# All differences of the experts' weights on DVE, and the token order spread over earlier steps

## The chip, the core and the metric

The kernel runs on one core of a Trainium2 chip. A core has a matrix engine (PE), three engines for elementwise work (DVE, ACT and POOL), a queue engine (SP) that issues most transfers, and 16 DMA engines. Each engine takes its instructions in the order in which they were written for it; a semaphore holds an instruction until what it needs is done, and everything behind it on that engine waits with it. The metric is the time of one execution in microseconds, the lower the better: 811.08 us is the median of three runs before the change.

## The reference, cut to what matters

```python
attn = softmax(scale * q @ k.T + alibi, causal, window=128)        # 4 x 8 heads x 576 x 64, fp32
x    = (attn @ v) as 2304 tokens x 512
e    = argmax(x @ w_gate)                                           # one of 8 experts per token
y    = gate * sigmoid(x @ w_output_gate)[e] * (relu(x @ w1[e]) @ w2[e])     # 512 -> 1024 -> 512
out  = (silu(y @ w_gate2) * (y @ w_val2)) @ w_out2                  # 512 -> 1536 -> 512, its weights are float64
```

All is computed to fp32 accuracy. Matmuls use a narrower format (fp32r), so each factor is split into a high part (a rounded copy) and a low part (the value minus its high part), and three products are added: high by high, high by low, low by high.

## The kernel before, in words

There are four stages: attention with the routing (to about 132 us of the span), a short stage of tables that sorts the experts by load, eight experts (145 to 381 us), and the last three matrices, called the wide stage (from 381 us).

The experts are numbered p = 0 to 7 by falling load. They take 384, 384, 352, 336, 304, 272, 256 and 256 tokens (the columns of their matmuls). Experts 0 to 6 run in one loop of 16 steps each: steps m = 0 to 7 make one eighth of the hidden layer each (12 matmuls into `oh`, L1441; ACT writes the high part `hh` with a Relu, L1449; DVE the low part `hl`, L1455), steps kk = 0 to 7 add one eighth of the second layer (12 matmuls into `oy`, L1465). Expert 7 does the same from lines of its own (`oh` L1235, `hl` L1247). In the steps kk = 0 to 5, `turn_step` makes the next expert's input: DVE transposes four blocks of tokens (`t<-xr`, L1090), ACT makes their high parts `xh` (L1097) and DVE their low parts `xl` (L1087); the block k is transposed at kk = k, and its `xl` stands at kk = k + 2, ahead of that step's other work. Expert 0's input is made with PE transposes instead (`emit_xT`; its `xl` is L1068). The first matmuls of an expert read all four blocks of `xh` and then all four of `xl`.

Behind each step, `behind_step` does two further jobs on the same engines:

- **Weights of the next expert and of the wide stage.** A *row* is a 128x512 block of an expert's weights: ACT makes its high part (L461) and the low part is a subtraction (L463), on POOL for every third row and on DVE for the others. 112 rows are done there, 37 of them on POOL. A *wide block* is a 128x256 block of float64, brought to fp32 by two ACT instructions (L405, L406) and two of DVE (L412, L417). From expert 1 on there is one row in each step and one wide block in each even step. Both come through a ring of seven staging tiles (`raw`, `rawd`), and SP issues the next load when one is given back.
- **One portion of the token order, in every second step.** `token_order` is a generator of 40 portions of small DVE instructions. Portions 1 to 29 make the list of where each token's result belongs; portions 15, 21 and 27 are six small PE matmuls each (`oid_ps`, L947), which read what DVE wrote in the portions 11 to 13, 17 to 19 and 23 to 25. Portions 30 to 40 make the tables for tokens over an expert's capacity; the last two issue a transfer from ACT's queue that waits for DVE (L1009, L1014). Portion k stands behind the loop's step 2k, counted from 1 over all experts: portion 40 is behind step 80, the last of expert 4.

The order on each engine is the order in which the program writes it (`manual_schedule`), so a portion or a row that is written earlier runs earlier on its engine.

Of the kernel before, what the change touches and what calls it, by code (L numbers as in the profile page):

```python
# [14 lines left out]
ALU = mybir.AluOpType  # L15
# [131 lines left out]
def attn_moe_glu_kernel(ctx, tc, q, k, v, w_gate, w_ogate, w1, w2, w2_gate, w2_val, w2_out, out, caps=CAPS):  # L147
    nc = tc.nc
# [65 lines left out]
    with ExitStack():  # L214
# [32 lines left out]
        def keep_warm(pool, tag, n):  # L247
# [11 lines left out]
            out=ident, in_=ident, pattern=[[-1, 128]], compare_op=ALU.is_equal, fill=0.0, base=0, channel_multiplier=1  # L259
# [29 lines left out]
        for h in range(H):  # L289
            nc.vector.tensor_scalar(  # L290
                out=bias[:, h, :], in0=dist, scalar1=-(2.0 ** (-8.0 * (h + 1) / H)) / scale, scalar2=None, op0=ALU.mult
# [97 lines left out]
        STEPS = 2 * KF  # L389
# [37 lines left out]

        wide_go = [False]

        loaded, halves, lows, n_rows = [], [], [], [0]  # L430
        sorted_known = [False]

        def w_load(most=LA):
# [23 lines left out]
        def w_item(eng):  # L457
            name, kk, c, t = loaded.pop(0)
            if c is None:
                s = slot_of(name, kk)  # L460
                nc.scalar.activation(out=s[:, 0, :], in_=t, func=AF.Copy)  # L461
                n_rows[0] += 1
                (nc.gpsimd if n_rows[0] % 3 == 0 else nc.vector).tensor_tensor(  # L463
                    out=s[:, 1, :], in0=t, in1=s[:, 0, :], op=ALU.subtract
                )
                wt[name + (kk,)] = s
            else:
                fp = 2 * name[2] + c
                if fp == len(wraw):
                    wraw.append(wB[0].tile([128, 2, 2 * KD, 128], I32, tag="wx", name="wraw", bufs=NX))  # L470
                narrow_merge(*narrow_act(t), wraw[fp][:, :, AT[name[0]][kk], :])
            w_load()
# [369 lines left out]
        def scratch():  # L842
# [5 lines left out]
        TT, TS, STT, RED = (  # L848
            nc.vector.tensor_tensor, nc.vector.tensor_scalar, nc.vector.scalar_tensor_tensor, nc.vector.tensor_reduce)
# [204 lines left out]
        def emit_xT(p, kks=range(KD)):  # L1054
            if p >= E:
                return
            n = caps[p]
            cb = -(-n // 128)
            r = xr[p]
            if p not in xe:  # L1060
                xe[p] = [grid(t, KD, n) for t in pair_tile(xe_p, "x", KD * cap)]
            xh, xl = xe[p]
            for kk in kks:
                t = ps_m.tile([128, CP], F32, tag="m", name="tx")
                for c in range(cb):
                    nc.tensor.transpose(t[:, c * 128:c * 128 + 128], features(r[:, c, 0:DM], kk), ident)
                nc.scalar.activation(out=xh[:, kk, :], in_=t[:, 0:n], func=AF.Copy)
                TT(out=xl[:, kk, :], in0=t[:, 0:n], in1=xh[:, kk, :], op=ALU.subtract)  # L1068
# [45 lines left out]
        step_no = [0]  # L1114
# [7 lines left out]
        def behind_step(i0=0):  # L1122
            for i in range(i0, len(plan[step_no[0]])):
                behind_item(i)
            step_no[0] += 1
            if step_no[0] % 2 == 0:
                next(tokens, None)

        UW = 2 * WU
# [294 lines left out]
        with tc.issue_after(last_cnt[0]):  # L1424
            keep_warm(ps_m, "m", 48)
        with tc.manual_schedule(engines=ALL_ORDERED):
            emit_xT(0)
            load_x(1)
            assert wn[0] == 8 and not loaded
            w_load()  # L1430
            tokens = token_order()
            for p in range(E - 1):
                n = caps[p]
                xh, xl = xe.pop(p)
# [1 line left out]
                for m in range(KF):  # L1436
                    o = ps_m.tile([128, cap], F32, tag="m", name="oh")
                    i = 0
                    for a, b in PASSES:
                        for kk in range(KD):  # L1440
                            nc.tensor.matmul(  # L1441
                                out=o[:, 0:n],
# [19 lines left out]
                for kk in range(KF):  # L1462
                    for d in range(KD):
                        for i, (a, b) in enumerate(PASSES):
                            nc.tensor.matmul(  # L1465
                                out=o[d][:, 0:n],
# [42 lines left out]
        with tc.For_i(0, n_ov, 1) as b:  # L1509
# [10 lines left out]
                out=xs[:, :], out_offset=bass.IndirectOffsetOnAxis(ap=pad[:, 0:1], axis=0), in_=xg[:, :],  # L1520
# [6 lines left out]
                out=w1t, in_=w1[bass.ds(e_r, 1)].rearrange("o (k p) f -> p (o k) f", p=128)  # L1527
# [93 lines left out]
```

## Time and profile before

| | |
|---|---|
| median of 3 runs (lowest, highest) | 811.08 us (810.14, 811.08) |
| the profiled execution, its span | 809.85 us, 808.1 us |
| PE busy | 780.0 us, 97% |
| DVE busy | 669.7 us, 83% |
| ACT busy | 504.9 us, 62% |
| POOL busy | 164.9 us, 20% |
| 16 DMA engines, hardware queue q1 | 45.4% |

The shares are averages over stages with different limits. PE is nearly always busy, so what the time can lose is what PE does not do at its peak: stretches in which it waits, and stretches in which its clock is granted at the lower of its two levels. For each of these one asks which engine ended the wait, and what that engine did in the microseconds ahead of it.

### The profile page before, as it was taken

Reading aid. Unit: us, or ns where it says so; the run is one execution under the profiler, and the core shown is the slowest. Engines: PE = TensorE matmul, PEld = TensorE weight load, DVE = VectorE, ACT = ScalarE, POOL = GpSimd, SP = SyncE. Lnnn points to the kernel's source line nnn. Section 1 sums busy time; section 2 is a strip of 40 time slices with the busy share of each in tenths; the row PEclk is TensorE's granted clock in tenths of the full one; section 3 lists DMA queues with packets and bytes.
Section 4 is the critical chain, followed back from the end, with each engine's and each line's share of the span. In section 5 each row is a group of like instructions: output and inputs, shape, how many; then the busy total and the mean of one; then the engine's idle time right before and its main releaser. Section 6 shows DMA issues by size and latency. Waiting matters only on the chain.

```text
span 808.1 us, 17509 instructions
## 1 busy us (share of the span) xinstructions
PE 780.0 (97%) x6031; PEld 724.3 (90%) x6031; DVE 669.7 (83%) x1771; ACT 504.9 (62%) x1355; POOL 164.9 (20%) x249
## 2 busy tenths in 40 slices
PE   8999998999999999899999999999999999999994
PEld 6888875899999999899899999999999999999993
DVE  7799888498887997889999999999877898777642
ACT  6999972356576657668776766665544665445521
POOL 5467886031121222210000000040000002000003
PEclk9999999999999999899999999999999999999997
DMA  9999943897888878891343321233110113011102
GB/s 183 239 216 301 287 146 119 259 301 247 247 231 265 260 226 251 277 305 45 127 135 105 105 92 52 64 119 131 53 52 27 53 54 131 27 52 53 53 27 81
DMA packets 120815, 121.16 MB, mean 150 GB/s; under 512 B 63634, under 2 KB 79634, under 8 KB 120722
## 3 DMA queue, kind: packets, MB, share of 16 engines
q1 hardware_dynamic: 113184, 106.31, 45.4%
q0 software_dynamic: 2880, 9.48, 3.1%
q10 hardware_dynamic: 4658, 4.20, 1.5%
q8 instruction: 49, 0.80, 0.4%
q14 instruction: 44, 0.36, 0.2%
HBM read 89.23 MB, written 30.73 MB: 148 GB/s over the span
## 4 chain that ended last, share of the span: by engine, by line
PE 50%; issue 33%; DVE 8%; DMA 2%; ACT 2%; POOL 2%; SPq 0%; ACTq 0%; another core or an unknown queue 0%; DVEq 0%; POOLq 0%
PE oh L1441 11%; PE oy L1465 9%; PE pa L1315 7%; PE oo L1338 6%; PE pb L1315 5%; PE o L615 3%; PE s L524 3%; POOL out_dram L1353 2%; PE tp L592 2%; PE tq L498 1%; PE oy L1256 1%; PE oh L1235 1%; DVE p L557 1%; DVE xtok L686 1%; DVE w L463 1%
## 5 line engine op out<-in xcount | busy, mean ns | idle before, releaser
L1338 PE MATMUL oo<-xh,hw 128*128 128x512 f32 x432 | 133.4, 390 | 0.0
L1315 PE MATMUL pa<-w 128*128 128x384 f32 x630 | 127.9, 338 | 0.8 <-ACT wtmp L1176 0.6
L1315 PEld LDWEIGHTS pa<-w 128*128 128x128 f32 x630 | 112.2, 188 | 9.4 <-ACT wtmp L1176 1.3
L1353 POOL DMA_INDIRECT out_dram<-ob,oid x18 | 20.5, 1138 | 419.0 <-ACT ob L1176 293.7
L1465 PE MATMUL oy<-hh,w 128*128 128x384 f32 (+5 forms) x448 | 101.1, 312 | 0.0
L1315 PE MATMUL pb<-w 128*128 128x384 f32 x468 | 94.5, 336 | 0.0
L1338 PEld LDWEIGHTS oo<-xh,hw 128*128 128x128 f32 x432 | 79.6, 188 | 6.4
L1176 ACT ACTIVATE w<-w 128x256 fp32r<-128x256 f32 (+2 forms) x168 | 76.1, 461 | 14.2 <-DVE w L1203 10.5
L463 POOL TENSOR_TENSOR w<-raw,w 128x512 fp32r<-128x512 f32 x37 | 49.9, 1348 | 170.2 <-ACT w L461 117.5
L1338 PE MATMUL oo<-xl,hw 128*128 128x512 f32 x216 | 84.4, 391 | 0.0
L1315 PEld LDWEIGHTS pb<-w 128*128 128x128 f32 x468 | 82.7, 188 | 0.4 <-DVE wtmp L1391 0.3
L1441 PE MATMUL oh<-xh,w 128*128 128x384 f32 (+5 forms) x448 | 81.0, 321 | 0.5 <-ACT xh L1097 0.5
L1176 ACT ACTIVATE wtmp<-pa 128x384 f32<-128x384 f32 x72 | 35.4, 492 | 64.9 <-PE pa L1315 64.7
L1465 PEld LDWEIGHTS oy<-hh,w 128*128 128x128 f32 x448 | 75.8, 188 | 0.0
L1441 PEld LDWEIGHTS oh<-xh,w 128*128 128x128 f32 x448 | 72.2, 197 | 1.2 <-ACT xh L1097 0.7
L461 ACT ACTIVATE w<-raw 128x512 fp32r<-128x512 f32 x112 | 67.7, 622 | 8.0 <-ACT y L1110 5.1
L1176 ACT ACTIVATE w<-wraw 128x256 fp32r<-128x256 f32 x108 | 44.4, 414 | 41.7 <-PE pa L1315 26.2
L1465 PE MATMUL oy<-hl,w 128*128 128x384 f32 (+5 forms) x224 | 69.8, 312 | 0.0
L1391 DVE TENSOR_TENSOR wtmp<-pb,wtmp 128x384 f32<-128x384 f32 x72 | 40.1, 557 | 32.3 <-ACT wtmp L1176 26.2
L1388 DVE TENSOR_TENSOR wtmp<-wtmp 128x384 f32<-128x384 f32 x108 | 58.6, 554 | 6.3 <-ACT wtmp L1394 5.7
L463 DVE TENSOR_TENSOR w<-raw,w 128x512 fp32r<-128x512 f32 x75 | 52.4, 706 | 5.2 <-ACT w L461 4.9
L578 ACT ACTIVATE p<-p,mn 128x128 f32<-128x128 f32 x144 | 56.1, 407 | 0.8 <-DVE mn L557 0.8
(259 smaller groups left out, 1683.1 us busy)
## 6 DMA issues: line engine op xcount, KB each, us to landing
raw<-in_moe_w_dram SPq DMA_DIRECT2D x128, 256.0 KB, 3.9
xs<-zrow SPq DMA_DIRECT2D x8, 774.0 KB, 7.6
rawd<-in_moe_w_gate_dram SPq DMA_DIRECT2D x24, 256.0 KB, 3.9
rawd<-in_moe_w_val_dram SPq DMA_DIRECT2D x24, 256.0 KB, 3.6
rawd<-in_moe_w_out_dram SPq DMA_DIRECT2D x24, 256.0 KB, 3.6
xh<-wo_s SPq DMA_DIRECT2D x24, 256.0 KB, 2.6
xl<-wo_s SPq DMA_DIRECT2D x24, 256.0 KB, 2.9
w<-ys SPq DMA_DIRECT2D x6, 768.0 KB, 7.5
```

What stands on the lines that cost most here:

```text
L461: nc.scalar.activation(out=s[:, 0, :], in_=t, func=AF.Copy)
L463: (nc.gpsimd if n_rows[0] % 3 == 0 else nc.vector).tensor_tensor(out=s[:, 1, :], in0=t, in1=s[:, 0, :], op=ALU.subtract)
L524: nc.tensor.matmul(out=sp[64 * qh:64 * qh + 64, a, pp, int(z == hi), c0:c1], lhsT=x[:, d, pp, 64 * qh:64 * qh + 64], rhs=x[:, z, 2 + pp, c ...
L578: last_exp[0] = nc.scalar.activation(out=pr[:, c, :], in_=pr[:, c, :], func=AF.Exp, bias=mn[:, c:c + 1], scale=-1.0, accum_out=sums[j][:, ...
L1176: nc.scalar.activation(out=out, in_=in_, func=AF.Copy)
L1315: nc.tensor.matmul(out=bank_of(j), lhsT=w[:, a, k, :], rhs=x_at(j, b, k), start=(n == 0 and j in (0, 1, 5)), stop=(n == 5), skip_group_che ...
L1338: nc.tensor.matmul(out=o_w[c], lhsT=h_at(s, t)[b][:, b0 * 128:b0 * 128 + 128], rhs=wo_at(s, a), start=(kk == 0 and i == 0), stop=(kk == KF ...
L1353: r = nc.gpsimd.indirect_dma_start(out=out[:, :], out_offset=bass.IndirectOffsetOnAxis(ap=oid[:, 2 * WB * pr + c, :], axis=0), in_=ob, in_ ...
L1388: TT(out=out, in0=a, in1=b, op=ALU.mult)
L1391: TT(out=temp(i), in0=bank_of(j), in1=temp(k), op=ALU.add)
L1441: nc.tensor.matmul(out=o[:, 0:n], lhsT=wt["w1", p, m // 4, kk][:, a, (m % 4) * 128:(m % 4) * 128 + 128], rhs=(xh, xl)[b][:, kk, :], start= ...
L1465: nc.tensor.matmul(out=o[d][:, 0:n], lhsT=wt["w2", p, 0, kk][:, a, d * 128:d * 128 + 128], rhs=(hh, hl)[b][:, kk, :], start=(kk == 0 and i ...
```

## The change: what it does

Two things. All 112 subtractions of the rows go to DVE, and POOL has none left. And the portions of the token order are written earlier: portions 1 to 5 ahead of `emit_xT(0)`, the input of expert 0; then one portion behind each of expert 0's 16 steps (portions 6 to 21); then one behind every second step as before (portion 27 behind step 28, portion 40 behind step 54, in expert 3). Lines behind the first edit have numbers lower by one to three.

```diff
@@ -459,10 +459,7 @@
             if c is None:
                 s = slot_of(name, kk)
                 nc.scalar.activation(out=s[:, 0, :], in_=t, func=AF.Copy)
-                n_rows[0] += 1
-                (nc.gpsimd if n_rows[0] % 3 == 0 else nc.vector).tensor_tensor(
-                    out=s[:, 1, :], in0=t, in1=s[:, 0, :], op=ALU.subtract
-                )
+                TT(out=s[:, 1, :], in0=t, in1=s[:, 0, :], op=ALU.subtract)
                 wt[name + (kk,)] = s
@@ -1123,7 +1120,7 @@
             for i in range(i0, len(plan[step_no[0]])):
                 behind_item(i)
             step_no[0] += 1
-            if step_no[0] % 2 == 0:
+            if step_no[0] <= STEPS or step_no[0] % 2 == 0:
                 next(tokens, None)
@@ -1424,11 +1421,13 @@
         with tc.manual_schedule(engines=ALL_ORDERED):
+            tokens = token_order()
+            for _ in range(5):
+                next(tokens)
             emit_xT(0)
             load_x(1)
             assert wn[0] == 8 and not loaded
             w_load()
-            tokens = token_order()
             for p in range(E - 1):
```

DVE at the start of the experts, before (`cape` is the last result of the stage of tables, `xl` the input of expert 0, `more` and `behind` are the first portions):

```order
L888 TENSOR_TENSOR tbl<-tbl,capt 128x64
L889 TENSOR_REDUCE cape<-tbl 128x8
L1068 TENSOR_TENSOR xl<-tx,xh 128x384 x4
L1455 SCALAR_TENSOR_TENSOR hl<-oh,hh 128x384 x2
L895 TENSOR_TENSOR more<-cnt,cape 128x8
L896 TENSOR_SCALAR more<-more 128x8
L897 COPY behind<-more 128x8
L899 TENSOR_TENSOR behind<-behind 128x1 x3
L1455 SCALAR_TENSOR_TENSOR hl<-oh,hh 128x384 x2
```

The same place now, from the end of portion 3 on (ahead of these rows stand portions 1 to 3):

```order
L902 TENSOR_TENSOR behind<-behind,total 128x8
L907 TENSOR_TENSOR tbl<-iota_74,expf 128x144
L909 TENSOR_TENSOR tbl<-tbl,offe 128x144
L910 TENSOR_REDUCE at<-tbl 128x18
L909 TENSOR_TENSOR tbl<-tbl,cape 128x144
L910 TENSOR_REDUCE lim_3087<-tbl 128x18
L1065 TENSOR_TENSOR xl<-tx,xh 128x384 x4
L1454 SCALAR_TENSOR_TENSOR hl<-oh,hh 128x384
L909 TENSOR_TENSOR tbl<-tbl,behind 128x144
L910 TENSOR_REDUCE far<-tbl 128x18
L1454 SCALAR_TENSOR_TENSOR hl<-oh,hh 128x384
```

19 instructions of the portions 1 to 5 now stand ahead of the four `xl`, and each step of expert 0 has a portion behind its `hl`.

DVE in expert 4's steps kk = 2 to 4, before (`xl` and `t` belong to the input of expert 5; `lack`, `row` and `first` are portions 37 and 38):

```order
L996 SCALAR_TENSOR_TENSOR first<-ib,first 128x17
L997 SCALAR_TENSOR_TENSOR first<-eb,first 128x17
L1087 TENSOR_TENSOR xl<-t,xh 128x272
L1090 STREAM_TRANSPOSE t<-xr 128x288
L463 TENSOR_TENSOR w<-raw,w 128x512
L412 SCALAR_TENSOR_TENSOR rawd<-rawd 128x256
L417 SCALAR_TENSOR_TENSOR wraw<-rawd 128x2x128
L1087 TENSOR_TENSOR xl<-t,xh 128x272
L1090 STREAM_TRANSPOSE t<-xr 128x288
L1002 TENSOR_TENSOR lack<-rest,tokid 128x17
L1003 TENSOR_TENSOR row<-first,tokid 128x17
L1004 SCALAR_TENSOR_TENSOR row<-row,lack 128x17
```

The same steps now:

```order
L1084 TENSOR_TENSOR xl<-t,xh 128x272
L1087 STREAM_TRANSPOSE t<-xr 128x288
L462 TENSOR_TENSOR w<-raw,w 128x512
L412 SCALAR_TENSOR_TENSOR rawd<-rawd 128x256
L417 SCALAR_TENSOR_TENSOR wraw<-rawd 128x2x128
L1084 TENSOR_TENSOR xl<-t,xh 128x272
L1087 STREAM_TRANSPOSE t<-xr 128x288
L462 TENSOR_TENSOR w<-raw,w 128x512
L1084 TENSOR_TENSOR xl<-t,xh 128x272
```

The portions are gone from here, and the row of step kk = 3, whose subtraction was POOL's, stands between the last transpose and the third `xl`.

## Rows read from the trace of the kernel before

**Rows 1.** Waits of PE: engine, line, releaser: us in total, times, longest.

```profile
PE oh L1441 <- DVE xl L1087: 4.3, 2, 2.7
...
PE oh L1441 <- ACT xh L1097: 0.5, 1, 0.5
```

**Rows 2.** Timeline of PE, start of expert 5: start, us, instruction, [idle before <- releaser].

```profile
300.09 0.79 PE L1441 MATMUL oh<-xh,w 128*128 128x272 f32 x4
...
303.00 0.40 PE L1441 MATMUL oh<-xl,w 128*128 128x272 f32 x1 [1.66 <-DVE xl L1087]
...
307.77 1.17 PE L1441 MATMUL oh<-xh,w 128*128 128x272 f32 x8
308.77 0.67 PE L1441 MATMUL oh<-xl,w 128*128 128x272 f32 x4
```

**Rows 3.** Timeline of PE, start of expert 6.

```profile
332.43 0.58 PE L1441 MATMUL oh<-xl,w 128*128 128x256 f32 x1 [2.66 <-DVE xl L1087]
...
337.93 1.25 PE L1441 MATMUL oh<-xh,w 128*128 128x256 f32 x8
```

**Rows 4.** Timeline of PE, start of expert 7.

```profile
359.69 0.39 PE L1235 MATMUL oh<-xl,w 128*128 128x256 f32 x1 [1.79 <-DVE xl L1087]
```

**Rows 5.** Windows: stretch, us, busy of PE, PEld, DVE, ACT, POOL, clock, DMA share, GB/s.

```profile
300.00:310.00 10.00, 8.34 (x52) 8.02 (x52) 5.59 (x16) 4.77 (x11) 1.28 (x1) 0.83 0.82 230
...
330.00:340.00 10.00, 7.57 (x42) 7.57 (x43) 7.75 (x15) 6.40 (x17) 2.69 (x2) 0.66 1.00 289
```

**Rows 6.** The page's groups: the rows' subtraction on POOL and on DVE.

```profile
L463 POOL TENSOR_TENSOR w<-raw,w 128x512 fp32r<-128x512 f32 x37 | 49.9, 1348 | 170.2 <-ACT w L461 117.5
...
L463 DVE TENSOR_TENSOR w<-raw,w 128x512 fp32r<-128x512 f32 x75 | 52.4, 706 | 5.2 <-ACT w L461 4.9
```

**Rows 7.** Timeline of POOL, around the last `xl` of expert 6's input.

```profile
330.69 1.41 POOL L463 TENSOR_TENSOR w<-raw,w 128x512 fp32r<-128x512 f32 x1 [4.02 <-ACT w L461]
```

**Rows 8.** Transfers of the stretch 300 to 360 us: packets, bytes, mean rate.

```profile
DMA packets 11232, 16.10 MB, mean 268 GB/s; under 512 B 1179, under 2 KB 5228, under 8 KB 11226
```

**Rows 9.** Timeline of DVE, from the start of expert 0 to expert 7.

```profile
144.74 1.95 DVE L1068 TENSOR_TENSOR xl<-tx,xh 128x384 fp32r<-128x384 f32 x4 [4.72 <-ACT xh L1067]
...
159.96 1.11 DVE L902 TENSOR_TENSOR behind<-behind,more 128x8 f32<-128x8 f32 x1
...
272.33 1.39 DVE L972 TENSOR_TENSOR tbl<-omore,lim 128x136 f32<-128x136 f32 x1
...
290.81 0.46 DVE L1455 SCALAR_TENSOR_TENSOR hl<-oh,hh 128x304 fp32r<-128x304 f32 x1
...
300.37 0.18 DVE L1005 TENSOR_SCALAR row<-row 128x17 f32<-128x17 f32 x1
...
302.51 0.43 DVE L1087 TENSOR_TENSOR xl<-t,xh 128x272 fp32r<-128x272 f32 x1
...
310.47 0.44 DVE L1455 SCALAR_TENSOR_TENSOR hl<-oh,hh 128x272 fp32r<-128x272 f32 x1 [2.82 <-ACT hh L1449]
...
321.12 0.43 DVE L1455 SCALAR_TENSOR_TENSOR hl<-oh,hh 128x272 fp32r<-128x272 f32 x1
...
330.87 1.50 DVE L1087 TENSOR_TENSOR xl<-t,xh 128x256 fp32r<-128x256 f32 x1
...
348.43 0.42 DVE L1455 SCALAR_TENSOR_TENSOR hl<-oh,hh 128x256 fp32r<-128x256 f32 x1
...
357.52 1.32 DVE L412 SCALAR_TENSOR_TENSOR rawd<-rawd 128x256 int32<-128x256 int32 x1 [0.74 <-ACT rawd L406]
...
359.22 0.42 DVE L1087 TENSOR_TENSOR xl<-t,xh 128x256 fp32r<-128x256 f32 x1
```

**Rows 10.** Timeline of DVE, the tightest of the earlier starts (expert 3).

```profile
239.79 1.60 DVE L1087 TENSOR_TENSOR xl<-t,xh 128x336 fp32r<-128x336 f32 x1
```

**Rows 11.** Timeline of PE, starts of expert 1 and expert 3.

```profile
178.92 0.86 PE L1441 MATMUL oh<-xh,w 128*128 128x384 f32 x4
...
244.03 0.78 PE L1441 MATMUL oh<-xl,w 128*128 128x336 f32 x4
```

More of the change, by code (lines that the diff above doesn't have):

```diff
@@ L428, in attn_moe_glu_kernel @@
         wide_go = [False]
-        loaded, halves, lows, n_rows = [], [], [], [0]
+        loaded, halves, lows = [], [], []
         sorted_known = [False]
```

## The prediction

> **What bounds the kernel now.** I read the page first (PE busy 97%, so little can be had), then the list of PE's waits, then PE's timeline at each wait, then DVE's timeline backwards from there. PE waits in three places that matter, all on `xl`, the low part of the next expert's input, which DVE makes [rows 1]: at the start of expert 5 for 1.66 us [rows 2], of expert 6 for 2.66 us and 0.5 for `xh` just ahead [rows 1, 3], of expert 7 for 1.79 us [rows 4], 6.6 us together. Two of them cost more than the wait. After the first, the 25 matmuls from 303.00 to 307.77 take 4.77 us, where eight at full rate take 1.00, 0.125 each [rows 2]: 25 x 0.125 = 3.1, so 1.65 us are lost. After the second, the 25 matmuls from 332.43 to 337.93 take 5.50 us, and at 0.125 x 256/272 = 0.118 each they would take 2.95 [rows 2, 3]: 2.55 us lost. The windows there show the granted clock at 0.83 and 0.66 of full speed [rows 5], thus partly at 1.2 GHz instead of 2.4. After the third wait there is no such stretch. In all PE loses 6.6 + 1.65 + 2.55 = 10.8 us, and that is about all this change can win: from 381 us on PE waits only twice, for 0.6 and 0.2 us, on wide-stage work that does not change.
>
> Why is `xl` late? DVE works without a pause from 271 to 303 us, then stands still 2.82 us [rows 9], then works without a pause to 332. The pause is of the kernel's own making: ACT's transfer of portion 40 waits for DVE and holds up the `hh` behind it, and with it DVE's first `hl` of expert 5 at 310.47.
>
> **The change, part 1: 37 subtractions from POOL to DVE.** Added: 37 x 0.706 = 26.1 us of DVE by their mean duration [rows 6]; from one instruction's start to the next's it is 0.60, so 22.2. Removed: something that the busy times hide. While POOL subtracts (1.35 us mean [rows 6]), a DVE instruction with two inputs in SBUF that starts in that time ends only about 0.3 us after POOL does: POOL runs from 330.69 to 332.10 and the `xl` begun at 330.87 takes 1.50 us [rows 7, 9], against 0.42 for the same shape with POOL idle (359.22 [rows 9]). `hl`, with one input in PSUM, and the transposes do not show it. Over all 37, the surplus of the DVE instruction beside each runs from nothing to 1.1 us, the first being 159.96 (1.11 for an instruction of 0.17), the last 357.52 (1.32 for 0.42) [rows 9], and adds up to 25.3 us. So DVE's total changes by -3 to +1 us; I take -1. The worst victims are `xl` themselves.
>
> The Trainium skill has a rule for this ("SBUF — State Buffer", section "SBUF: two separate sides"): the port pair shared by VectorE and GpSimd is an exclusive lock, and whichever starts first makes the other wait in full. The trace agrees. Another page of the Trainium skill ("Trainium Architecture — The Big Picture", section "What this means for kernel authors") says that the engines are independent processors; taken alone, without the exception that it makes for that pair, DVE would have 22 to 26 us more to do and get nothing back. The rows with a surplus speak against that.
>
> Each row moved into a stretch counts +0.60 us for DVE, each surplus there is subtracted. SP's next load waits for the subtraction, now behind DVE's queue and no longer behind POOL's 1.35 us: I cost that at nothing, since DVE does it within 1 to 2 us; without that cover ACT would wait for loads.
>
> **Part 2: the portions.** Ahead of expert 0, 19 small instructions of 0.15 to 0.35 us start to start, about 4.4 us, go into 4.72 us in which DVE waits for the input [rows 9]; an overrun of 0.9 is still hidden, because PE first has four matmuls with `xh`. Expert 0 gets portions 6 to 21 where it had 1 to 8. In its first half DVE waits for PE in most steps, which takes the first of them; adding up the instructions of the second half, DVE passes portion 19 some 2 us before PE asks for it (the `oid_ps` matmuls now at that expert's end, 178.92 [rows 11]). Expert 2 gets portions 30 to 37, heavier than the 17 to 24 it had. Its end is the tightest of the early ones: the last `xl` is done at 239.79 + 1.60 = 241.4 [rows 10] and PE needs it three matmuls into 244.03, at 244.5 [rows 11], 3.1 us spare. Portions 34 and 35 add 2.3 us there, two rows 1.2; the surpluses of 0.55 and 1.1 go; with what the first half carries over I get 1.5 us spare. Expert 3 has portions 38 to 40, whose two transfers block ACT for about 2.5 us; I estimate 1.5 us spare at its end too.
>
> Experts 4 and 5 lose all portions: 28 instructions from 272.33 to 300.37 [rows 9], 8.0 us of DVE start to start, and the blocked ACT.
>
> *Start of expert 5.* Before, the last `hl` ends at 291.27 and the last `xl` at 302.94: 11.7 us [rows 9]. Now take away portions 36 to 38 (1.45) and a surplus of 1.1, add two rows (1.2): 10.3. The last `hl` itself comes 2.3 us earlier, at 289, since 5.9 us of portions in front are gone and then the Relu (287.9) sets it. So the last `xl` is there at 299.3, and PE needs it seven matmuls after 300.09 [rows 2], at 301.0. The wait goes, with 1.7 us to spare, and its slow stretch: 3.3 us won.
>
> *Start of expert 6.* PE's halves of expert 5 are 96 x 0.125 = 12.1 us each. Let X be the end of the first; ACT, with two stores of results in that half, finishes the last Relu 1.4 us after X and DVE the last `hl` 2.4 us after. From there to the last `xl` it took 332.37 - 321.55 = 10.8 us [rows 9]; surpluses of 0.2, 0.6 and 1.1 go, two rows come (1.2): 10.1. That is X + 12.5; PE needs X + 12.1 + 0.8 = X + 12.9. The wait goes, with 0.4 us to spare: up to 2.66 + 0.5 + 2.55 = 5.7 won.
>
> *Start of expert 7.* Before, 359.64 - 348.85 = 10.8 us from the last `hl` [rows 9]; surpluses of 0.55 and 0.9 go, two rows come, one of them into the 0.74 us in which DVE waits at 357.52 [rows 9]: 9.9 to 10.5. Done at X + 12.4 to 12.9; PE's half is 96 x 0.118 = 11.3, so it needs X + 12.1. A wait of 0.3 to 0.8 stays, I take 0.6 of the 1.79.
>
> **DMA.** The stretch from 300 to 360 us moves 16.1 MB, 268 GB/s in the mean [rows 8], and would now have 10 us less, 322 GB/s. So loads will come late at times. Bound from below: nothing, since the share is 0.82 at 230 GB/s in one window, short of full [rows 5], and peaks may even out; from above: if the 289 GB/s at share 1.00 [rows 5] is all there is, 16.1 MB take 55.7 us instead of 50.2: 5.5. I take 1 us, nearer to nothing, because the last of these loads are the wide stage's and can wait, and seven staged tiles ride over short peaks.
>
> The Trainium skill ("DMA: Bandwidth & Descriptors", "Specifications") gives about 358 GB/s from HBM for a core; by that figure, an estimate, 16.1 MB would take 45 us, nothing would wait and the sum would be 1 us lower. The row with share 1.00 at 289 GB/s speaks for less, at least in the window in which the loads of `xr` in small pieces fall.
>
> **The sum.** 10.8 - 0.6 - 1 = 9.2, and with DVE's 1 us less in all nothing more, as it lies beside PE. The profiled execution took 809.85: 800.6 after. It was 1.2 us under the median of 811.08, so against the medians: 811.1 - 9.2 = 801.9; I say 801.8.
>
> **The rivals.**
> - *Expert 6 still waits.* Spare time there is only 0.4 us. For: ACT is full in that half, and loads get denser. If it waits 1 us or more, the clock falls too: about 1 + 2.3 stay, and expert 7's 1.2 more. Won: 5 to 6. Time 804 to 807. The same time comes from DMA at its upper bound (801.8 - 1 + 5.5 = 806.3).
> - *Only the portions count.* If the surpluses are not all given back, the rows add 1.2 at each start: expert 6 then waits 1.6 and keeps its slow stretch, expert 7 waits 2.3. Won: about 3.5. Time 807.5.
> - *Slower: DVE's extra rows are real.* If what stretches DVE's instructions is not POOL, DVE has 22 us more in order. Expert 3 then waits 0.4 (3.1 - 2.3 - 1.2) and 4 about 0.6, both with a slow stretch of 1.6; 5 waits 0.3 + 1.6; 6 waits 1.6 + 2.7; 7 waits 2.3 + 2.5: 15.2 lost against 10.8 now, 815.5. It decides where the spare 3.1 us at expert 3 are used up. For it: POOL was idle 80% of the time; against it: 34 of the 37 have a stretched DVE instruction beside them.
> - *No change:* DMA sets the pace of the whole stage, and what DVE gives back turns into waits for loads. Against it: ACT's waits for weights come to 0.3 us from 300 to 335 us. Time 810 to 811.
>
> **How the numbers follow.** Forecast 0.53 (799.5 to 804); expert 6 still waiting or DMA 0.24; only the portions 0.08; no change 0.06; slower 0.09. The range reaches from all of the 10.8 (and a little DVE time) to the second case and the start of the third: 799.3 to 807.5. Of this kernel 0.2%, or 1.6 us, can be told from no change. Faster 0.84, same 0.06, slower 0.10.
>
> **What would show it.** In the profile after: POOL without L463 groups; DVE's `xl` at its shortest duration everywhere (0.42 to 0.55); no wait on `xl` at expert 5, none or under 0.5 at 6, under 1 at 7; no window of the experts with a clock under 0.9 behind 150 us; DVE's total within 3 us. I am wrong if a wait stands at expert 3 or 4, if PE waits for the `oid_ps` portion at 179, or if ACT waits for `raw` loads from 310 on.

## The result, and the profile after

The changed kernel takes 803.83 us (median of 4 runs, 802.85 to 805.16) against 810.80 for the kernel before beside it (4 runs, 810.14 to 811.08), so 7.0 us less by the medians where 9.3 were forecast. The ratio on record is 0.9904, with a 95% interval of 0.9887 to 0.9920; the quotient of the two medians, 0.9914, lies inside it. The profiled execution took 804.16 us with a span of 802.0. Run twice more, on two chips, each time with the kernel before beside it, the changed kernel gave ratios of 0.9918 (0.9900 to 0.9936) and 0.9938 (0.9919 to 0.9957), by the medians 6.5 and 4.8 us less.

PE's waits on `xl` in the changed kernel, the answer to [rows 1] (its lines stand 3 lower: L1440 was L1441, L1084 was L1087, L1454 was L1455):

```profile
PE oh L1440 <- DVE xl L1084: 1.6, 1, 1.6
...
PE oh L1232 <- DVE xl L1084: 1.2, 1, 1.2
```

Of three waits two are left, and the 0.5 us on `xh` ahead of expert 6 is gone too. PE's timeline at the starts of experts 5, 6 and 7, against [rows 2 to 4]:

```profile
302.75 0.66 PE L1440 MATMUL oh<-xh,w 128*128 128x272 f32 x4
...
329.76 0.38 PE L1440 MATMUL oh<-xl,w 128*128 128x256 f32 x1 [1.59 <-DVE xl L1084]
329.98 1.71 PE L1440 MATMUL oh<-xh,w 128*128 128x256 f32 x8
...
334.34 1.10 PE L1440 MATMUL oh<-xh,w 128*128 128x256 f32 x8
...
355.37 0.39 PE L1232 MATMUL oh<-xl,w 128*128 128x256 f32 x1 [1.21 <-DVE xl L1084]
```

Expert 5 starts without a pause, expert 7 behind a wait of 1.21 us. At expert 6 PE waits 1.59 us, and the eight matmuls behind the wait take 1.71 us instead of the 1.10 at 334.34. The window there shows it too, against [rows 5]; the columns are the same:

```profile
310.00:320.00 10.00, 10.00 (x82) 10.00 (x81) 8.32 (x19) 8.31 (x21) 0.00 (x0) 1.00 0.98 327
...
330.00:340.00 10.00, 10.00 (x74) 10.00 (x74) 7.71 (x17) 6.99 (x19) 0.00 (x0) 0.83 1.03 308
```

The granted clock is 0.83 from 330 to 340 us; split into single microseconds it is 0.50, the 1.2 GHz level, from 331 to 333. The page's group of the row subtractions, against [rows 6]:

```profile
L462 DVE TENSOR_TENSOR w<-raw,w 128x512 fp32r<-128x512 f32 x112 | 75.1, 678 | 8.2 <-ACT w L461 6.6
```

POOL has none left. DVE's total went from 669.7 to 667.0 us, although 75.1 - 52.4 = 22.7 us of subtractions came to it; so 25.4 us of other DVE time went, which is the 25.3 that the prediction added up as surpluses.

To compare executions I cut each profile at two points: expert 0's first matmul, and the first of the wide stage (`pb`). In between lies all that the change moves, but for the five portions ahead of expert 0. That stage took 381.59 - 145.03 = 236.6 us before and 377.27 - 147.61 = 229.7 after: 6.9 less. (Outside it, expert 0 began 2.6 us later in the profile after, and the stretch from the last matmul to the end was 1.7 us shorter. When the kernel before was run again, below, it began at 147.3 and ended in the same time as the changed one, so neither is put down to the change.)

### The profile page after: what moved, and what is told of

Read it like the earlier page. It is cut to its first block, busy times and chain, and to the rows that moved or that the text cites. A ratio compares the mean times of both kernels' runs of the same rounds, so it can differ in the third digit from the quotient of the medians.

```text
span 802.0 us, 17462 instructions
## 1 busy us (share of the span) xinstructions
PE 777.6 (97%) x6031; PEld 720.7 (90%) x6031; DVE 667.0 (83%) x1808; ACT 504.7 (63%) x1355; POOL 115.2 (14%) x212
## 4 chain that ended last, share of the span: by engine, by line
PE 40%; issue 34%; DVE 11%; ACT 6%; DMA 4%; POOL 2%; ACTq 1%; DVEq 0%; POOLq 0%; SPq 0%
PE pa L1312 7%; PE oo L1335 6%; PE oh L1440 5%; PE pb L1312 5%; PE oy L1464 4%; PE o L612 3%; DVE w L462 2%; PE s L521 2%; POOL out_dram L1350 2%; DMA rawd<-in_moe_w_gate_dram 2%; ACT w L461 2%; PE tp L589 1%; PE oy L1253 1%; PE oh L1232 1%; DVE t L1087 1%
## 5 line engine op out<-in xcount | busy, mean ns | idle before, releaser
L462 DVE TENSOR_TENSOR w<-raw,w 128x512 fp32r<-128x512 f32 x112 | 75.1, 678 | 8.2 <-ACT w L461 6.6
L1440 PE MATMUL oh<-xh,w 128*128 128x384 f32 (+5 forms) x448 | 79.1, 316 | 0.0
L1440 PEld LDWEIGHTS oh<-xh,w 128*128 128x128 f32 x448 | 70.5, 192 | 0.6 <-ACT xh L1064 0.4
L1221 DVE TENSOR_TENSOR w<-wraw,w 128x256 fp32r<-128x256 f32 x108 | 44.3, 419 | 6.3 <-ACT w L1173 6.3
```

The lines of the kernel that those rows point to most:

```text
L462: TT(out=s[:, 1, :], in0=t, in1=s[:, 0, :], op=ALU.subtract)
L1221: TT(out=flat(w_at(s, j)[:, 1]), in0=w_src(s, j), in1=flat(w_at(s, j)[:, 0]), op=ALU.subtract)
L1440: nc.tensor.matmul(out=o[:, 0:n], lhsT=wt["w1", p, m // 4, kk][:, a, (m % 4) * 128:(m % 4) * 128 + 128], rhs=(xh, xl)[b][:, kk, :], start= ...
```

## The experiments

The table has every run. "Stage" is as above. The last three columns say how much longer PE's first half of experts 5, 6 and 7 was than without any wait (12.0, 11.3 and 11.3 us, from the run in which nothing waits). The ratio is to the kernel before, run beside the version. The letter is the chip: the runs stand in three groups, A, B and C, on one chip each; the first two profiles have no chip on record.

| kernel | ratio (95%) | expert 0 starts at | stage, us | 5 | 6 | 7 |
|---|---|---|---|---|---|---|
| before | | 145.0 | 236.6 | 3.7 | 6.4 | 2.1 |
| before again (e10, C) | 0.9991 (0.9976-1.0007) | 147.3 | 236.1 | 2.8 | 5.6 | 3.1 |
| changed | 0.9904 (0.9887-0.9920) | 147.6 | 229.7 | 0.0 | 3.8 | 1.5 |
| changed (e8, B) | 0.9918 (0.9900-0.9936) | 147.2 | 233.6 | 1.2 | 2.0 | 5.8 |
| changed (e11, C) | 0.9938 (0.9919-0.9957) | 148.6 | 231.5 | 0.1 | 2.3 | 4.6 |
| rows only (e1, A) | 0.9948 (0.9934-0.9963) | 143.9 | 233.4 | 0.6 | 3.1 | 4.7 |
| portions only (e2, A) | 0.9987 (0.9971-1.0002) | 145.3 | 234.7 | 1.5 | 1.8 | 5.0 |
| all rows on POOL (e3, A) | 1.0183 (1.0156-1.0211) | 144.7 | 254.9 | 4.4 | 6.1 | 7.7 |
| none ahead (e4, B) | 0.9922 (0.9899-0.9945) | 149.8 | 232.6 | 1.7 | 1.9 | 4.6 |
| stores on POOL (e5, A) | 0.9894 (0.9872-0.9917) | 145.2 | 226.9 | 0.0 | 0.0 | 2.5 |
| stores on POOL (e12, C) | 0.9895 (0.9877-0.9914) | 147.5 | 227.1 | 0.0 | 0.0 | 2.7 |
| wide pieces early (e6, B) | 0.9894 (0.9876-0.9911) | 147.7 | 228.9 | 1.8 | 0.1 | 1.1 |
| both (e7, B) | 0.9867 (0.9845-0.9890) | 147.2 | 224.4 | 0.0 | 0.0 | 0.0 |
| both, old portions (e9, C) | 0.9895 (0.9877-0.9913) | 148.3 | 226.1 | 1.0 | 0.4 | 0.4 |

**Rows only.** The kernel before with

```
-                n_rows[0] += 1
-                (nc.gpsimd if n_rows[0] % 3 == 0 else nc.vector).tensor_tensor(
-                    out=s[:, 1, :], in0=t, in1=s[:, 0, :], op=ALU.subtract
-                )
+                TT(out=s[:, 1, :], in0=t, in1=s[:, 0, :], op=ALU.subtract)
```

> All 112 subtractions of rows on DVE, the portions where they were before. Theory (POOL's subtraction blocks DVE, so that moving it costs DVE nothing in sum): DVE's total stays within 3 us of 669.7, every xl takes 0.41 to 0.55 us; the start of expert 5 still waits 1.5 to 1.8 us (one surplus of 1.1 gone, two rows of 0.6 come, ACT still stands behind portion 40's transfers), that of expert 6 about 2.0 instead of 2.66, that of expert 7 about 1.2 instead of 1.79; ratio to before 0.996 to 1.000. Rival (the stretched DVE instructions have another cause): DVE's total rises by 22 to 26 us, waits at experts 3 to 7, ratio 1.005 or more. Second rival (the rows are the main part of the gain): ratio 0.993 or less.

DVE's total is 667.0 us and the total of surpluses is gone, as the theory said; the ratio is 0.9948, 4.2 us less, beyond the theory's 0.996 and short of the second rival's 0.993. Two starts miss. Expert 7 waits 1.11 us for `xh` and 1.58 for `xl`, where 1.2 were expected (1.79 and 2.46 for `xl` in the two profiles of before). Expert 5 waits 0.26 us, where 1.5 to 1.8 were expected. PE's timeline of this run at expert 5, and DVE's last `xl` ahead of it:

```profile
298.92 0.66 PE L1438 MATMUL oh<-xh,w 128*128 128x272 f32 x4
...
300.21 0.39 PE L1438 MATMUL oh<-xl,w 128*128 128x272 f32 x1 [0.26 <-DVE xl L1084]
```

```profile
277.87 0.47 DVE L1452 SCALAR_TENSOR_TENSOR hl<-oh,hh 128x304 fp32r<-128x304 f32 x1 [0.25 <-ACT hh L1446]
...
299.72 0.43 DVE L1084 TENSOR_TENSOR xl<-t,xh 128x272 fp32r<-128x272 f32 x1
```

Why so little is left of that wait is in DVE's timeline of the kernel before, in the stretch in which it never pauses. Four blocked instructions there count:

```profile
280.28 0.97 DVE L412 SCALAR_TENSOR_TENSOR rawd<-rawd 128x256 int32<-128x256 int32 x1
...
286.52 1.28 DVE L989 TENSOR_TENSOR tbl<-tbl,omore 128x136 f32<-128x136 f32 x1
...
289.48 1.41 DVE L417 SCALAR_TENSOR_TENSOR wraw<-rawd 128x256 int32<-128x256 int32 x1
...
297.73 1.53 DVE L1087 TENSOR_TENSOR xl<-t,xh 128x272 fp32r<-128x272 f32 x1
```

(A fifth, at 272.33 [rows 9], lies ahead of the pause at 277.87 above, in which DVE now waits for `hh`; what it gave back ends in that pause.) With POOL idle the four take 0.43, 0.30, 0.43 and 0.43: 3.6 us of surplus. Four rows at 0.60 take their place, 2.4. So the rows alone bring DVE forward by 1.2 us, and I had counted the last surplus alone (-1.1) against two rows (+1.2). Measured, the last `xl` ends 1.23 us after expert 5's first matmul (299.72 + 0.43 - 298.92) instead of 2.85 (302.94 - 300.09): 1.6 us earlier, 0.4 more than this count.

**Portions only.** The changed kernel with

```
-                TT(out=s[:, 1, :], in0=t, in1=s[:, 0, :], op=ALU.subtract)
+                n_rows[0] += 1
+                (nc.gpsimd if n_rows[0] % 3 == 0 else nc.vector).tensor_tensor(
+                    out=s[:, 1, :], in0=t, in1=s[:, 0, :], op=ALU.subtract
+                )
```

> Every third row's subtraction on POOL as before, the portions moved as in the changed kernel. Theory (each part alone leaves a wait and a slow stretch at expert 6, so that the two together are worth more than the sum): expert 5 starts without a wait over 0.5 us, expert 6 waits 2 us or more with a slow stretch behind it, expert 7 1.5 to 2.3 us; ratio 0.994 to 0.997. Rival (the portions are all of it, POOL's rows do not matter): ratio 0.990 to 0.992, as with both parts. In both the stretch before expert 1 is asked as well: in the profile of the changed kernel expert 1 began 3.0 us later than before, 2 of them lost in the attention around 95 us; if that comes with the change, it is there in this run too, if it is one execution's own, not in all runs.

Neither came. The gain of 1.0 us by the ratio (2.3 by the medians) is less than the 2.4 to 4.9 of the theory, and no change lies within the interval; the rival's 0.990 to 0.992 is far off. Expert 6 waits 1.51 us (2 or more expected) and expert 7 2.46, but expert 5 waits 1.17 instead of under 0.5, and experts 3 and 4 now wait 0.51 and 1.18, where the portions went. The sum of the two single parts is 0.52 + 0.13 = 0.65%, both together 0.62 to 0.96% on the record's three pairs: they support each other by 0 to 0.3%, no more can be told. That the move of the portions pays at all is not shown by any pair alone: the interval of rows only (0.9934 to 0.9963) overlaps that of the changed kernel in its third run (0.9919 to 0.9957). All pairs point the same way.

**All rows on POOL.** The changed kernel with

```
-                TT(out=s[:, 1, :], in0=t, in1=s[:, 0, :], op=ALU.subtract)
+                nc.gpsimd.tensor_tensor(out=s[:, 1, :], in0=t, in1=s[:, 0, :], op=ALU.subtract)
```

> The changed kernel with all 112 rows' subtractions on POOL and none on DVE: the dose raised from 0 to three times that of before. Theory (a subtraction on POOL takes about as much DVE time by blocking as the same subtraction on DVE takes in itself): DVE's total stays within 10 us of 667 although 112 x 0.67 = 75 us of work are gone from it, xl and other instructions with two inputs in SBUF take up to 1.6 us each; no faster than the changed kernel, ratio to before 0.993 to 1.010. Rival (no blocking): DVE's total falls by 60 to 75 us, to 592 to 607, no waits on xl, ratio 0.988 or less.

The theory holds, and nearly its size: DVE's total is 677.3 us, 10.3 above the changed kernel's where up to 10 were allowed, although 75.1 us of subtractions are gone from it. The ratio is 1.0183, more than the 1.010 that I allowed: the blocked `xl` come late, and PE waits for them 2.7 to 4.3 us at the start of each of the experts 3 to 7. The groups of DVE in the changed kernel, from 147 to 400 us (columns as on the page, shapes apart):

```profile
L412 DVE SCALAR_TENSOR_TENSOR rawd<-rawd 128x256 int32<-128x256 int32 x52 | 22.0, 423 | 0.5 <-ACT rawd L406 0.4
...
L1454 DVE SCALAR_TENSOR_TENSOR hl<-oh,hh 128x384 fp32r<-128x384 f32 x16 | 8.9, 556 | 11.1 <-ACT hh L1448 11.1
L1087 DVE STREAM_TRANSPOSE t<-xr 128x352 f32<-128x352 f32 x8 | 6.4, 803 | 0.1
...
L938 DVE TENSOR_SCALAR tbl<-iota,far 128x128 bf16<-128x128 bf16 x18 | 3.7, 249 | 0.0
...
L1084 DVE TENSOR_TENSOR xl<-t,xh 128x384 fp32r<-128x384 f32 x4 | 2.2, 553 | 0.0
```

and with all rows on POOL:

```profile
L412 DVE SCALAR_TENSOR_TENSOR rawd<-rawd 128x256 int32<-128x256 int32 x49 | 44.8, 915 | 25.2 <-ACT rawd L406 23.8 <-issue 1.3
...
L938 DVE TENSOR_SCALAR tbl<-iota,far 128x128 bf16<-128x128 bf16 x18 | 17.0, 985 | 0.0
L1454 DVE SCALAR_TENSOR_TENSOR hl<-oh,hh 128x384 fp32r<-128x384 f32 x16 | 8.8, 553 | 11.1 <-ACT hh L1448 11.1
L1087 DVE STREAM_TRANSPOSE t<-xr 128x352 f32<-128x352 f32 x8 | 6.4, 805 | 0.1
...
L1084 DVE TENSOR_TENSOR xl<-t,xh 128x384 fp32r<-128x384 f32 x4 | 4.7, 1183 | 0.0
```

The same instructions take 915 instead of 423 ns, 985 instead of 249, 1183 instead of 553, while `hl` (one input in PSUM) and the transposes do not change. The Trainium skill ("SBUF — State Buffer", section "Who interferes with whom") names just these kinds: two inputs in SBUF, or copy, cast and tensor_scalar in a mode that uses both ports; the trace agrees.

**The changed kernel again**, without an edit.

> The changed kernel once more, nothing edited. In its first profile expert 0 began at 147.6 us, in the five others between 143.9 and 145.3, and from the last matmul to the end of the span it took 10.3 us, in the profile of before 12.2. Theory (these two belong to an execution, not to the change): expert 0 begins between 143.5 and 146, while the stretch from its first matmul to the start of the wide stage is 229.7 us within 0.5, as in the first profile (236.6 before), with the waits of about 1.6 us at expert 6 and 1.2 at 7. Rival (the attention is late with this program): expert 0 at 147 or later again. Ratio to before 0.989 to 0.993 in either.

Expert 0 began at 147.2, outside the theory's 143.5 to 146 (the kernel before again, below, has more on it); the stage took 233.6, outside 229.7 +- 0.5. PE's timeline at experts 6 and 7 of this execution:

```profile
330.43 0.39 PE L1440 MATMUL oh<-xl,w 128*128 128x256 f32 x1 [1.59 <-DVE xl L1084]
330.66 1.10 PE L1440 MATMUL oh<-xh,w 128*128 128x256 f32 x8
...
356.16 0.58 PE L1232 MATMUL oh<-xl,w 128*128 128x256 f32 x1 [1.59 <-DVE xl L1084]
356.54 1.91 PE L1232 MATMUL oh<-xh,w 128*128 128x256 f32 x8
```

The same wait of 1.59 us at expert 6 is followed by full clock here (1.10) and by half clock in the first profile (1.71); at expert 7 it is the other way round, though there the waits differ too (1.21 us in the first profile, 0.89 and 1.59 here). What a wait costs behind itself is not fixed, and one profile of this stage is good to about 2 us either way (229.7, 233.6 and 231.5 in the three of this kernel).

**None ahead.** The changed kernel with

```
-            for _ in range(5):
-                next(tokens)
```

> The changed kernel without the five portions ahead of expert 0: portions 1 to 16 in its steps, then one in every second, the last in expert 3's last step instead of 11 steps earlier. Theory (what counts is that experts 4 and 5 are free of portions): waits at experts 5 to 7 as in the changed kernel, the one at expert 4 between 0 and 1 us because portion 40's transfer now holds ACT at its end; ratio to before 0.989 to 0.993. Rival (the front part is what brings it): losses of over 2 us at experts 4 and 5, ratio 0.993 to 0.996.

0.9922 and no wait at expert 4: as the theory has it. The five portions ahead bring nothing that these runs can tell from zero.

**Stores on POOL's queue.** The changed kernel with

```
-                nc.scalar.dma_start(out=rows[:, 0:n_p] if p == 0 ...
+                nc.gpsimd.dma_start(out=rows[:, 0:n_p] if p == 0 ...
```

and the offsets' `value_load` on the same engine.

> The changed kernel with the stores of experts 0 to 5's results issued from POOL's queue instead of ACT's. Theory (the last hl of expert 5 ends 5.0 us after the first half instead of 2.4 because ACT is late, and each of the stores holds ACT for about 1.1 us, of which 0.35 is the issue and about 0.5 a wait for its own copy): ACT's last Relu of expert 5 comes 1.5 to 2 us earlier, the wait of 1.59 us at expert 6 and its slow stretch of 1.2 us go, that at expert 7 (1.2) shrinks to 0.3 to 1.0; ratio to before 0.985 to 0.988 (2 to 4 us under the changed kernel). Rival (the loads set ACT's pace: it waited 0.96 us for a load at 310.5): the waits for loads grow by what the stores give back, the start of expert 6 still waits 1 us or more; ratio 0.990 to 0.992 as without the edit. Second rival: the issue on POOL blocks or delays DVE, slower than the changed kernel.

The wait at expert 6 is gone and the clock stays full; but expert 7's did not shrink, it lost 2.5 us. So theory and rival are each right at one place, and the ratio lies between theirs. The second rival is out: DVE's total is 667.2 us, as in the changed kernel. Repeated beside the changed kernel:

> The changed kernel with the stores issued from POOL's queue, now beside the changed kernel on one chip. Theory (the stores make ACT late and with it the start of expert 6): expert 6 starts without a wait again and the last hl of expert 5 ends 2 us behind the first half; what is left is expert 7; 1.5 to 5 us less than the changed kernel's median of this call, stage 226 to 229 us. Rival (the first run of this edit was a lucky one): a wait of 1 us or more at expert 6, and the medians within 1 us.

803.74 against 807.04 us, 3.3 less, and stage 227.1 against 231.5. DVE's last `hl` of expert 5, and PE at the starts of experts 6 and 7, in this run:

```profile
315.75 0.43 DVE L1454 SCALAR_TENSOR_TENSOR hl<-oh,hh 128x272 fp32r<-128x272 f32 x1
```

```profile
326.68 0.64 PE L1440 MATMUL oh<-xh,w 128*128 128x256 f32 x4
327.15 0.63 PE L1440 MATMUL oh<-xl,w 128*128 128x256 f32 x4
...
350.30 0.39 PE L1232 MATMUL oh<-xh,w 128*128 128x256 f32 x1 [0.49 <-ACT xh L1094]
...
352.74 0.38 PE L1232 MATMUL oh<-xl,w 128*128 128x256 f32 x1 [1.59 <-DVE xl L1084]
```

PE's first half of expert 5 ends at 314.63, so the last `hl` is there 1.55 us later. At expert 7 ACT's waits for loads show up, from 296 to 332 us:

```profile
ACT rawd L405 <- DMA rawd<-in_moe_w_gate_dram: 3.0, 2, 2.7
```

**Wide pieces early.** The changed kernel with

```
+        WIDE_N = (0, 11, 9, 9, 8, 6, 5, 0)
...
-            if st >= STEPS and st % 2 == 0 and left_h:
+            if st % STEPS * WIDE_N[st // STEPS] % STEPS < WIDE_N[st // STEPS] and left_h:
```

> The changed kernel with the 48 pieces of the wide weights laid 11, 9, 9, 8, 6 and 5 into the steps of experts 1 to 6 instead of 8 into each, which takes 5 loads of 256 KB and 5 x 0.85 us of DVE out of experts 5 and 6 and puts them into 1 to 3. Theory (by expert 5 the steps are short and the loads, ACT and DVE late together): the start of expert 6 waits less than 0.5 us, that of expert 7 less than 0.5; waits of ACT for loads from 300 us on go; no new wait over 0.5 us at experts 2 to 4; 228.5 us or less of wait-free work from expert 0 to the wide stage would be 224.4, I expect 224 to 226.5 against 229.7; ratio to before 0.984 to 0.988. Rival (the last portions in experts 2 and 3 leave no room): waits of 1 us or more at the start of expert 3 or 4, ratio 0.988 to 0.994.

Expert 6 is right (0.1 us lost), but experts 4 and 5 lose 1.4 and 1.8 us behind waits of 0.36 + 0.58 and 1.44: the rival's mechanism, one expert later than it said. Expert 7 waits 0.74 us, over the 0.5 expected. The stage took 228.9 us where 224 to 226.5 were expected, and the ratio, 0.9894, is above the theory's range and no better than moving the stores.

**Both.** The two diffs above together.

> The wide pieces laid as in the run before and the stores on POOL's queue. If the pieces alone take all waits, the same time as that run (within 0.15%); if ACT's stores still cost something, 1 to 2 us less; PE starts experts 5, 6 and 7 without a wait; ratio to before 0.983 to 0.987. The rival is the DMA load that turned up at expert 7 when the stores left ACT: a wait of 1 us or more there again, 0.987 to 0.990.

No wait is left in the stage, and the clock is full in every window (columns as in [rows 5]):

```profile
330.00:340.00 10.00, 10.00 (x87) 10.00 (x87) 7.38 (x18) 7.15 (x19) 1.08 (x2) 1.00 0.97 320
...
350.00:360.00 10.00, 10.00 (x88) 10.00 (x87) 6.40 (x13) 4.51 (x11) 0.00 (x0) 1.00 0.67 241
```

800.88 us against 805.18 for the changed kernel, 802.97 with the pieces alone and 811.71 for the one before, all on chip B: this version beats both kernels, and the stores are still worth 2.1 us beside the pieces. The stage is 9.2 us shorter than in the neighbouring profile and the medians 4.3 apart. Part of the difference is at the end: from the last matmul to the end of the span it takes 12.3 to 12.8 us in all four profiles with stores on POOL's queue, 10.2 to 10.7 in all others but the first one of before, where it takes 12.0 with no store on POOL's queue. What causes it was not tried.

**Both, with the portions where they were.** That version with

```
-            if step_no[0] <= STEPS or step_no[0] % 2 == 0:
+            if step_no[0] % 2 == 0:
...
-            for _ in range(5):
-                next(tokens)
```

> The version without any wait (all rows on DVE, stores on POOL's queue, wide pieces 11, 9, 9, 8, 6, 5) with the portions back where they were before: none ahead, one behind every second step, the last five in experts 4 and 5. It asks whether the portions' move is still needed. Theory (DVE has no room for 8 us of portions in experts 4 and 5, and portion 40's transfers hold ACT): waits of 0.3 to 2 us at expert 5 and of 1 us or more at expert 6, stage 226.5 to 230 us against 224.4, ratio to before 0.988 to 0.992. Rival (with the pieces moved there is room): no wait over 0.3 us, stage 224 to 225, ratio 0.984 to 0.988.

Expert 5 waits 0.57 us as the theory has it, expert 6 loses only 0.4; stage 226.1, just under its range. By these two profiles the move is still worth 1.7 us of stage there, less than I thought; that is within what one profile is good to, and the intervals of the two ratios (0.9845 to 0.9890 and 0.9877 to 0.9913) overlap, so it is not shown.

**The kernel before again**, without an edit.

> The kernel before once more, for a profile taken beside those of the changed kernel. Theory (when expert 0 begins depends on the session, not on the change): expert 0 begins within 1 us of where it begins in the changed kernel's profile of this call. Rival (the change makes the attention end later): 1.5 us or more ahead of it. The stage from expert 0's first matmul to the wide stage: 236.6 us in the first profile; between 233.5 and 238 if the losses behind waits vary as much as in the changed kernel (229.7 and 233.6).

Expert 0 began at 147.3, 2.3 us later than in the first profile of the same kernel, and 1.35 before the changed kernel's 148.6, between what theory and rival said. The table settles more of it. On chip A expert 0 begins at 143.9 to 145.3, on B at 147.2 to 149.8, on C at 147.3 to 148.6; the same edits began at 145.2 on A and 147.5 on C (the stores'). The start goes with the chip or the session, and the two cannot be told apart here. Nor do the five portions ahead of expert 0 move it one way: the version without them is the earliest on A by 0.8 us or more, the latest on B by 2.1, and on C the two without stand among the two with.

**The changed kernel a third time**, without an edit.

> The changed kernel a third time, as the neighbour of the two runs that follow. Ratio to before 0.989 to 0.993; the stage from expert 0 to the wide stage between 229 and 234 us, with 1.6 us of wait at expert 6 and 1 us or more at expert 7.

The stage took 231.5 us and PE waited 1.59 at expert 6 and 1.04 + 1.59 at expert 7, as expected; the ratio, 0.9938, is a little above the 0.993 that I gave.

## Why the prediction was nearly right, and which step failed

- *Subtractions cost DVE nothing in sum* (-3 to +1 us, -1 taken): right, -2.7 measured (665.5 to 667.0 us in the three profiles of the changed kernel, 669.3 and 669.7 before); all on POOL shows the same law at three times the dose. `xl` takes 0.41 to 0.43 us in the two widths of the late experts.
- *Experts 0 to 4 keep their slack*: right, no wait at 3 or 4, and none on the `oid_ps` matmuls at 181.8. The 1.7 us said to be spare at expert 5 were 0.3 (last `xl` at 303.3, needed at 303.6), and in e8 a wait of 0.97.
- *Which part pays*: wrong. I gave the rows 1 us and the surpluses at three starts, and took "only the portions" for worth 3.5. Alone, the rows brought 4.2 us and the portions 1.0. A queue that never idles carries every surplus behind it to the next deadline; I counted only those behind the last `hl`.
- *Start of expert 6*: this is the step that failed. It put ACT's last Relu at X + 1.4, the last `hl` at X + 2.4 and the last `xl` at X + 12.5, with 0.4 us to spare. X is 314.75. DVE's timeline of the changed kernel:

```profile
319.39 0.43 DVE L1454 SCALAR_TENSOR_TENSOR hl<-oh,hh 128x272 fp32r<-128x272 f32 x1
...
329.29 0.42 DVE L1084 TENSOR_TENSOR xl<-t,xh 128x256 fp32r<-128x256 f32 x1
```

The last `hl` ends at X + 5.1 (4.8 and 5.1 in the other two profiles), the last `xl` 9.9 us later, where 10.1 were forecast. So the chain behind `hl` was sized rightly and its start was not. It is the same at all three starts. How long after PE's first half of the expert ahead the last `hl` ends, in us:

| start of | before | forecast | changed (three profiles) | stores on POOL (two) | both |
|---|---|---|---|---|---|
| expert 5 | 4.5 | 2.2 | 3.7, 5.1, 4.0 | 1.9, 1.4 | 3.1 |
| expert 6 | 5.7 | 2.4 | 5.1, 4.8, 5.1 | 2.0, 1.6 | 2.5 |
| expert 7 | 3.2 | 2.4 to 2.5 | 3.5, 5.2, 5.3 | 4.6, 4.8 | 2.3 |

ACT's timeline of expert 5's first half says why:

```profile
304.15 0.41 ACT L1107 ACTIVATE y<-oy 128x304 f32<-128x304 f32 x1
304.87 0.35 ACTq L1109 DMA_DIRECT2D ys<-y  x1
305.32 0.43 ACT L1107 ACTIVATE y<-oy 128x304 f32<-128x304 f32 x1 [0.77 <-DVE wraw L417]
306.50 0.34 ACTq L1109 DMA_DIRECT2D ys<-y  x1
306.88 0.40 ACT L1448 ACTIVATE hh<-oh 128x272 fp32r<-128x272 f32 x1 [1.13 <-DMA xr<-xs]
...
310.50 0.63 ACT L461 ACTIVATE w<-raw 128x512 fp32r<-128x512 f32 x1 [0.96 <-DMA raw<-in_moe_w_dram]
...
312.96 0.42 ACT L1107 ACTIVATE y<-oy 128x304 f32<-128x304 f32 x1
313.42 0.34 ACTq L1109 DMA_DIRECT2D ys<-y  x1
313.80 0.63 ACT L461 ACTIVATE w<-raw 128x512 fp32r<-128x512 f32 x1 [0.41 <-ACT y L1107]
...
315.27 0.40 ACT L1107 ACTIVATE y<-oy 128x304 f32<-128x304 f32 x1
315.70 0.34 ACTq L1109 DMA_DIRECT2D ys<-y  x1
316.37 0.63 ACT L461 ACTIVATE w<-raw 128x512 fp32r<-128x512 f32 x1 [0.69 <-ACT y L1107]
...
318.37 0.38 ACT L1448 ACTIVATE hh<-oh 128x272 fp32r<-128x272 f32 x1
```

The prediction counted two stores in that half; there are four. From the start of its copy to the next instruction a store keeps ACT 1.17, 1.56, 0.84 and 1.10 us, 4.7 together. The first two hold up the first Relu: it starts 4.1 us after the half's first matmul, against 1.7 with the stores on POOL's queue. A load came 0.96 late; the last Relu ends at X + 4.0. With the stores on POOL's queue the four copies take 1.3 us of ACT, the last Relu ends at X + 0.8 and X + 0.6, and the wait is gone in both runs, which shows the stores as the cause here: 4.7 - 1.3 = 3.4 us is about the whole way from X + 4.0 to X + 0.6. A late load is there in some executions only (none in that half in e8, 0.4 us in e11). Why the first two stores hold ACT longer was not tried; their issue comes 0.3 and 0.8 us after the copy's end.

The rows of before had it already: there the last `hl` ended at 321.12 + 0.43 [rows 9], and PE's first half at 315.82, so X + 5.7. I put that lateness down to the two transfers of portion 40 and took nearly all of it away (X + 2.4); 0.7 us of it went. The pause read from [rows 9] is not all theirs either. DVE stood still twice there, 1.80 us ahead of 305.43 and 2.82 ahead of 310.47, and in ACT's timeline of before two stores stand between the second transfer (issued at 307.69) and the Relu:

```profile
308.31 0.42 ACT L1110 ACTIVATE y<-oy 128x304 f32<-128x304 f32 x1 [2.40 <-DVE er L1013]
...
309.19 0.43 ACT L1110 ACTIVATE y<-oy 128x304 f32<-128x304 f32 x1 [0.46 <-ACT y L1110]
...
310.04 0.40 ACT L1449 ACTIVATE hh<-oh 128x272 fp32r<-128x272 f32 x1 [0.42 <-PE oh L1441]
```

They take 1.7 us of that pause, and the change leaves them in place.

- *Start of expert 7* (0.3 to 0.8, 0.6 taken): the same step, and more than a size. From the last `hl` to the last `xl` it took 9.9 us as forecast, but `hl` came late, and PE waited 1.21, 0.89 + 1.59 and 1.04 + 1.59 us in the three profiles. With the slow stretch PE lost 1.5, 5.8 and 4.6 us there, against 2.1 and 3.1 before: in two of three it got worse. The stores alone do not explain it, as `hl` is late without them on ACT too (4.6 and 4.8), while ACT waits 2.0 and 2.7 us for one load. Only with both edits is it early (2.3); what makes it late in the changed kernel stays open.
- *The slow stretches and DMA*: all losses at the three starts were 12.2 us before, not 10.8. After, they were 5.2 (3.8 + 1.5), where 0.6, and 1 for DMA, were forecast; 12.2 - 5.2 = 7.0 is the whole difference of the stage (6.9). In the other two profiles they were 9.0 and 7.0, against 11.5 in the second one of before. The 289 GB/s of the upper bound were not all there is: the window above moved 327.
- *The signs of being wrong*: one came, as ACT waited 0.96 us for a `raw` load at 310.5. Of what the profile after was to show, three things failed: the waits at experts 6 (1.59, under 0.5 expected) and 7 (1.21, under 1), and the window with a clock of 0.83.
- *The rivals*: "Expert 6 still waits", with 804 to 807, is what happened: its place, its wait of 1 us or more and the slow stretch; the time is just under it, and in the other two runs in it (805.18 and 807.04). So the time lies in the stated range because the range took this rival in; that it came within about 2 us of the forecast is in part luck, as the gain was split wrongly between the parts, and in the other two runs it was 6.5 and 4.8 us.

## What to carry to other kernels

Count the surplus of a blocked engine over the whole stretch in which its queue does not pause, not only behind the last deadline. When a change removes one cause of a lateness that the trace shows, price that cause by itself and leave the rest of the lateness standing; what each engine issues to its queue (here a store, 0.8 to 1.6 us of ACT) belongs to the rest. And where a stall can cost clock or not, take several profiles before a difference of 2 us is explained.

## What the runs showed that I had not expected

- A DVE instruction with one tensor input is blocked too: the 128x128 bf16 tensor_scalar takes 985 instead of 249 ns beside POOL's subtractions.
- The same 1.59 us wait of PE costs 2.0 us in one execution and 3.8 in another, as the clock falls to 0.50 or stays.
- In the four profiles with the stores on POOL's queue the end of the program takes 2 us longer than in most others, 460 us after the last of them; that they are the cause is not shown.
